# Three buffers for the splits of the down sums, their places, two units' sums in the FFN phase, and three halves of one input on VectorE

## The chip, the cores and the metric

The kernel runs on one core of a Trainium2 chip. The metric is the device time of one execution in microseconds; a kernel's time is the median of several runs. TensorE (PE) multiplies, VectorE (DVE), ScalarE (ACT) and GpSimd (POOL) work elementwise, and SyncE (SP) issues nearly all transfers. Each engine works its instructions off in the order in which the program gives them.

## The reference

Three steps follow one another: strided attention (4 batches, 8 heads, 576 positions, head size 64), a mixture of 8 experts whose gate is balanced by eight Sinkhorn rounds, and an FFN with a sigmoid gate. All in float32; the 2304 tokens are the rows of `x`, which are 512 wide.

```
def _moe_ref(x, w_gate, w1, w2):
    ...                                  # P: gate, balanced over tokens and experts
    for e in range(E):                   # E = 8, w1[e] 512 x 1024, w2[e] 1024 x 512
        h = np.maximum(x @ w1[e], 0.0)
        ye = h @ w2[e]
        out += P[:, e:e + 1] * ye

def _moe2_ref(x, w_in, w_out):           # 512 x 2048 and 2048 x 512
    h = x @ w_in
    g = h * (1.0 / (1.0 + np.exp(-1.702 * h)))
    return (g @ w_out).astype(np.float32)
```

## The kernel before, in words

**Blocks and phases.** The tokens are cut into three blocks of 768. The work behind the attention goes through six phases: MoE of block 0 (phase 0), MoE of block 1 (phase 1), FFN of block 0 (phase 2), MoE of block 2 (phase 3, "seven"), FFN of block 1 (phase 4), FFN of block 2 (phase 5). A phase is cut into units of 256 hidden columns: 32 units in a MoE phase (four an expert), 8 in an FFN phase. So units 0 to 31 are phase 0, 32 to 63 phase 1, 64 to 71 phase 2, 72 to 103 phase 3, 104 to 111 phase 4 and 112 to 119 phase 5.

**Products.** Float32 accuracy is had by splitting each operand into a high half (rounded to float32r by ScalarE) and a low half (the difference, made by GpSimd or VectorE), and adding three products. The product of a unit with its up weights is done by a scheme of seven smaller products in place of eight (PRODUCTS: X11, S1, S2, X12, S3, S4, X22), each six matmuls of 384 columns into a bank A, B or C. S1 to S4 are sums of quarters of the input (tiles `sa`, `sb`), T1 to T4 are sums of quarters of the weight. ScalarE copies some partial results out of the bank before the next product adds into it (`c`); after X11 that copy has to be done before product S2 goes on adding into bank A.

**Pieces.** A unit is 13 pieces: product 0, down tile 0, product 1, down tile 1 and so on to product 6. A down tile is six matmuls of 512 columns with the hidden values of the unit before. `side[piece_at(unit, k)]` holds the work of the other engines that is issued right behind piece k of a unit; a k of 13 or more is a piece of the next unit. Within one piece the order is that of the calls that filled it: `plan_weights` and `plan_inputs` come first, `plan_down_sums` late. The whole order is written out by hand; the tile framework only adds the waits.

**The weights of phase 3.** In phase 3 the down product too is done by the scheme of seven, and its weights come from a DRAM buffer `s7moe` (`sw7`), which is filled in phase 1. There `plan_down_sums` makes for every unit, from the down weights that the unit has loaded anyway (`raw`), four sums T1 to T4 on GpSimd (tile `dsums`, pieces 6 and 7), and splits each: high half on ScalarE, low half on GpSimd (tile `kw`, two buffers), then a store to `s7moe` by SyncE, one split at each of the pieces 8 to 11. A buffer of `kw` is free once its store has landed.

**Inputs of the next phase.** `plan_inputs` makes the split input `xc` of a phase during the last two units of the phase before: high halves on ScalarE, low halves on GpSimd; those numbered 1, 3 and 5, and the sums S3 and S4, are on VectorE for the phases of block 0 (`shared`). In phases 2 and 3 the results of the MoE are turned (`px`, four TensorE transposes and a ScalarE copy) into the input of a later FFN phase.

**FFN of block 0.** In phase 2 the FFN weights are new: GpSimd makes the four weight sums of the next unit (three instructions, L205 to L207) and the low halves of seven weight tiles and two down-weight tiles a unit, ScalarE their high halves. Later phases load them split.

**Phase 3's end.** Unit 104 carries its seven products and the last fourteen chains of phase 3's down product, whose inputs `comb` are split by ScalarE, VectorE and GpSimd and whose results VectorE adds into `sum`.

Of the kernel before, what the change touches and what calls it, by code (L numbers as in the profile page):

```python
# [8 lines left out]
F32 = mybir.dt.float32  # L9
F32R = mybir.dt.float32r  # L10
# [5 lines left out]
P = 128  # L16
# [26 lines left out]
PRODUCTS = (  # L43
    ("X11", "W11", "A", True, False),
    ("S1", "T1", "C", True, False),
    ("S2", "T2", "A", False, False),
    ("X12", "W21", "B", True, True),
    ("S3", "T3", "A", False, False),
    ("S4", "W22", "C", False, True),
    ("X22", "T4", "A", False, True),  # L50
)
NPR = len(PRODUCTS)
# [3 lines left out]
def strided_attention_moe_ffn(  # L56
# [13 lines left out]
    nc = tc.nc  # L70
    B, NPAIR, _, _, S = qk.shape
    NT, D = out.shape
# [25 lines left out]
    raws = ExitStack()  # L98
# [49 lines left out]
    side = defaultdict(list)  # L148
# [11 lines left out]
    FIRST_UNIT = []  # L160
# [10 lines left out]
    def seven(i):  # L171
        return S0 <= i < S1
# [4 lines left out]
    def piece_at(unit, k):  # L177
        return unit * PPU + k


    raw = {}
# [83 lines left out]

    SEVEN_FROM = NB - 2
    down_sums = {}

    def plan_down_sums(dp, i):

        n = UNITS[i][3]
        g = nc.gpsimd

        def q(k):
            return raw[2, i][:, k // 2, k % 2 * 2 * P : (k % 2 + 1) * 2 * P]

        def sums(m):
            if m == 0:
                down_sums[i] = dp.tile([P, 4, 2 * P], F32, tag="sums", name="dsums")
            t = down_sums[i]  # L280
            a, b = ((q(1), q(0)), (q(3), q(1)), (q(3), t[:, 0, :]), (q(2), t[:, 2, :]))[m]
            g.tensor_tensor(out=t[:, m, :], in0=a, in1=b, op=ALU.subtract)  # L282

        def split(k):
            t = dp.tile([P, 2, 2 * P], F32R, tag="kw", name="kw", bufs=2)
            src = down_sums[i][:, WHERE[PRODUCTS[k][1]][1], :]
            split_into(t, src, sw7[n, k].rearrange("p (h c) -> p h c", h=2))

        for m in range(4):
            side[piece_at(i, 6 + m // 2)].append(lambda m=m: sums(m))  # L290
        ks = [k for k in range(NPR) if PRODUCTS[k][1][0] == "T"]
        for m, k in enumerate(ks):
            side[piece_at(i, 8 + m)].append(lambda k=k: split(k))

    def plan_weights():

# [19 lines left out]
    def plan_sums(dp, i, lo, hi):  # L316

        r = {}

        def load():  # L320
            r["raw"] = dp.tile([P, 4, 2 * P], F32, tag="raws", name="raws")
            nc.sync.dma_start(out=r["raw"].rearrange("p q c -> p (q c)"), in_=wa[UNITS[i][3]])

        def sums():
            raw[1, i] = r["raw"]
            r["todo"] = sums_w1(i, dp)

        def split(k):
            t = dp.tile([P, 2, 2 * P], F32R, tag="kw", name="kw", bufs=2)
            split_into(t, quarter(i, PRODUCTS[k][1]), sw1["moe"][UNITS[i][3], k].rearrange("p (h c) -> p h c", h=2))  # L330

        tasks = [load, lambda: None, sums] + [lambda n=n: r["todo"][n]() for n in range(4)]
        tasks += [lambda k=k: split(k) for k in range(NPR) if PRODUCTS[k][1][0] == "T"]
        spread(tasks, lo, hi)
# [101 lines left out]
    def plan_inputs():  # L436

        v, g = nc.vector, nc.gpsimd
        for ph in range(1, len(PHASES)):
            last = FIRST_UNIT[ph] - 1  # L440

            shared = PHASES[ph][1] == 0
            low_v = (1, 3, 5) if shared else ()

            def put(unit, k, fn, *args):
                side[piece_at(unit, k)].append(lambda: fn(*args))

            put(last - 1, 6, input_sum, ph, 1, g)
            put(last - 1, 8, input_sum, ph, 2, g)
            put(last - 1, 9, input_high, ph, 0)  # L450
            put(last - 1, 10, input_low, ph, 0, v if 0 in low_v else g)
            for m in range(1, NPR):
                put(last, 2 * m - 1, input_high, ph, m)
                put(last, 2 * m - 1, input_low, ph, m, v if m in low_v else g)
                if m in (1, 2):
                    put(last, 2 * m, input_sum, ph, m + 3, v if shared else g)
# [152 lines left out]
    at = {p: [i for i, x in enumerate(groups) if x[:2] == p] for p in pairs}  # L609
# [480 lines left out]
    with tc.manual_schedule():  # L1090

        idle = hp.tile([P, NH], F32R, tag="hh22", name="idle", bufs=2)
        nc.vector.memset(f(idle), 0.0)
        idle_out = ps.tile([P, 512], F32, tag="y", name="idle_out", bufs=2)

        def keep_warm(n):
            for _ in range(n):
                nc.tensor.matmul(out=idle_out[:, :NH], lhsT=idle[:, :P], rhs=idle, start=True, stop=True)

        load_qk(0, PAIRS[0])  # L1100
        keep_warm(IDLE_FIRST)
        nc.scalar.dma_start(out=msk, in_=masks)
        load_qk(0, PAIRS[1])
        load_v(0, PAIRS[0])
        nc.scalar.dma_start(out=cst, in_=consts)
        load_w1(0)
        load_w2(0)
        nc.vector.memset(wgr, 0.0)
        nc.sync.dma_start(out=wgr[:, :, :E], in_=wg)

        plan_weights()
        plan_inputs()
        plan_kept()
        plan_turns()

        done = [0]

        def advance():
            g = done[0]
            pieces[g]()  # L1120
            for t in side.pop(g, ()):
                t()
            done[0] += 1

        quota = [0.0]
        load_w1(1)
        ahead = defaultdict(list)
        QUARTERS = ("W21", "W11", "W22", "W12")
        for n, what in enumerate(QUARTERS):
            ahead[5 + 2 * n].append(lambda what=what: split_plain(0, what))  # L1130
            ahead[12 + n].append(lambda what=what: split_plain(1, what))
        for ft in range(2):
            ahead[10 + ft].append(lambda ft=ft: split_w2(0, ft))
            ahead[17 + ft].append(lambda ft=ft: split_w2(1, ft))
        ahead[12].append(lambda: load_w1(2))
        ahead[12].append(lambda: load_w2(1))

        ahead[10].append(lambda: split_input(3))
        ahead[NHALF + 3].append(lambda: split_input(0))
        ahead[22].append(lambda: split_input(6))  # L1140
        ahead[NFIRST + 3].append(lambda: split_input("X21"))
        BY_HALF = 4 * PLAIN + 3 * (PLAIN - 1)

        def fill_first():
            quota[0] += IDLE_GAP
            keep_warm(int(quota[0]))
            quota[0] -= int(quota[0])

        def fill_half():
            quota[0] += RATE_HALF  # L1150
            if quota[0] >= 1 and done[0] < BY_HALF:
                advance()
                quota[0] -= 1
            else:
                keep_warm(1)

        def fill():
            quota[0] += RATE
            while quota[0] >= 1:
                advance()  # L1160
                quota[0] -= 1

        plan_first_sums()
        side[20].append(lambda: gate_logits(0))
        for i in range(NSTEP):
            if i == NHALF + 4:
                quota[0] = 0.0
            att_step(i, fill_first if i < NHALF + 4 else fill_half if i < NFIRST + 4 else fill)
            for t in ahead.pop(i, ()):
                t()  # L1170

        while done[0] // PPU % 2 or done[0] % PPU < 2:
            advance()
        early.close()
        late.append(ctx.enter_context(tc.tile_pool(name="late", bufs=1, space=bass.MemoryType.PSUM)))
        turn_of.clear()
        dp = raws.enter_context(tc.tile_pool(name="dp", bufs=1, reuse_waits="tile"))
        g = done[0]
        steps = gate_steps()
        assert g + len(steps) + 2 < piece_at(WAITING * UPE + 1, 0), (g, len(steps))  # L1180
        for n, s in enumerate(steps):
            side[g + n].append(s)
        plan_decode(dp, g + len(steps), piece_at(FIRST_UNIT[2] - 4, 0))
        for i in range(PLAIN):
            plan_sums(dp, i, piece_at(WAITING * UPE + 4 + 6 * i, 0), piece_at(WAITING * UPE + 9 + 6 * i, 0))
        for i in range(FIRST_UNIT[1], FIRST_UNIT[2]):
            plan_down_sums(dp, i)
        plan_seven()
        while done[0] < piece_at(S0, 0):
            advance()  # L1190
        raws.close()
        sp.append(ctx.enter_context(tc.tile_pool(name="sp", bufs=1, reuse_waits="tile")))
        while done[0] < len(pieces):
            advance()
# [81 lines left out]
```

## Time and profile before

| | |
|---|---|
| time, median of 3 runs | 2060.83 us (2059.45 to 2063.22) |
| profiled execution | 2060.84 us, its span 2059.1 us |
| TensorE busy | 1988.2 us (97%) |
| VectorE busy | 1359.1 us (66%) |
| GpSimd busy | 1181.9 us (57%) |
| ScalarE busy | 815.9 us (40%) |
| moved by transfers | 483.41 MB, mean 235 GB/s |

All times in rows are microseconds from the start of the span, unless marked ns. A row of the timeline shows an instruction's start, its duration, its engine and line, what it writes and reads, and in brackets how long the engine stood idle before it and what ended that. PEclk is the granted clock of TensorE as a share of 2.4 GHz.

### The profile page before, as it was taken

Reading aid. Unit: us, or ns where it says so; the run is one execution under the profiler, and the core shown is the slowest. Engines: PE = TensorE matmul, PEld = TensorE weight load, DVE = VectorE, ACT = ScalarE, POOL = GpSimd, SP = SyncE. Lnnn points to the kernel's source line nnn. Section 1 sums busy time; section 2 is a strip of 40 time slices with the busy share of each in tenths; the row PEclk is TensorE's granted clock in tenths of the full one; section 3 lists DMA queues with packets and bytes.
Section 4 is the critical chain, followed back from the end, with each engine's and each line's share of the span. In section 5 each row is a group of like instructions: output and inputs, shape, how many; then the busy total and the mean of one; then the engine's idle time right before and its main releaser. Section 6 shows DMA issues by size and latency. Waiting matters only on the chain.

```text
span 2059.1 us, 32151 instructions
## 1 busy us (share of the span) xinstructions
PE 1988.2 (97%) x10697; PEld 1784.7 (87%) x10697; DVE 1359.1 (66%) x2427; ACT 815.9 (40%) x2014; POOL 1181.9 (57%) x1201
## 2 busy tenths in 40 slices
PE   8999999999999999999999899999999999999999
PEld 6777789888988888888888779899999999888888
DVE  6776587888876666666665556665656666566656
ACT  6555434444443333333333355433333333333432
POOL 4465557888887555555555776665555555830300
PEclk9999999999999999999999999999999999999999
DMA  6355468687766888888887676687788788665653
GB/s 211 121 171 203 155 209 272 220 274 248 254 202 225 277 279 277 283 282 263 281 278 256 223 251 244 202 296 257 245 268 266 260 264 259 220 192 179 209 186 132
DMA packets 245684, 483.41 MB, mean 235 GB/s; under 512 B 25824, under 2 KB 56720, under 8 KB 244752
## 3 DMA queue, kind: packets, MB, share of 16 engines
q1 hardware_dynamic: 245232, 480.91, 70.6%
q8 instruction: 85, 1.39, 0.3%
q14 instruction: 79, 0.65, 0.1%
q10 hardware_dynamic: 288, 0.46, 0.1%
HBM read 322.91 MB, written 158.36 MB: 234 GB/s over the span
## 4 chain that ended last, share of the span: by engine, by line
PE 73%; POOL 8%; DMA 6%; DVE 5%; ACT 4%; issue 3%; SPq 1%; ACTq 0%; POOLq 0%; DVEq 0%
PE pA L719 19%; PE y L879 11%; PE pC L719 9%; PE y L950 8%; PE y L952 8%; PE y L951 8%; PE pB L719 5%; DMA s7moe<-kw 5%; POOL w L219 2%; POOL dsums L282 2%; POOL xc L423 2%; POOL kw L219 1%; ACT hh L755 1%; PE sc L496 1%; DMA s7moe<-w 1%
## 5 line engine op out<-in xcount | busy, mean ns | idle before, releaser
L719 PE MATMUL pA<-xc,w 128*128 128x384 f32 x2880 | 575.2, 339 | 35.9 <-ACT c L745 34.1
L719 PEld LDWEIGHTS pA<-xc,w 128*128 128x128 f32 x2880 | 508.2, 189 | 70.8 <-ACT c L745 47.9
L950 PE MATMUL y<-w,hh 128*128 128x512 f32 x1056 | 418.5, 396 | 10.3 <-DVE acc L969 3.8
L952 PE MATMUL y<-w,hl 128*128 128x512 f32 x1056 | 420.5, 398 | 1.4 <-DVE hl L758 0.7
L951 PE MATMUL y<-w,hh 128*128 128x512 f32 x1056 | 418.2, 396 | 0.2 <-POOL w L219 0.2
L219 POOL TENSOR_TENSOR w<-raw,w 128x256 fp32r<-128x256 f32 (+1 forms) x266 | 286.8, 1084 | 227.1 <-ACT w L218 198.8
L969 DVE SCALAR_TENSOR_TENSOR acc<-y,pr,acc 128x512 f32<-128x512 f32 x300 | 224.3, 748 | 168.3 <-PE y L952 167.2
L719 PE MATMUL pC<-xc,w 128*128 128x384 f32 x1464 | 296.2, 336 | 0.0
L879 PE MATMUL y<-comb,w 128*128 128x384 f32 x1344 | 269.2, 335 | 5.0 <-POOL comb L829 3.0
L719 PEld LDWEIGHTS pC<-xc,w 128*128 128x128 f32 x1464 | 259.4, 188 | 16.0 <-issue 0.7
L879 PEld LDWEIGHTS y<-comb,w 128*128 128x128 f32 x1344 | 236.7, 188 | 5.6 <-POOL comb L829 3.4
L952 PEld LDWEIGHTS y<-w,hl 128*128 128x128 f32 x1056 | 198.7, 188 | 47.0 <-DVE hl L768 2.7
L950 PEld LDWEIGHTS y<-w,hh 128*128 128x128 f32 x1056 | 199.3, 189 | 42.1 <-ACT hh L765 5.4
L951 PEld LDWEIGHTS y<-w,hh 128*128 128x128 f32 x1056 | 198.9, 188 | 25.1 <-POOL w L219 0.6
L829 POOL TENSOR_TENSOR comb<-s,comb 128x384 fp32r<-128x384 f32 x128 | 129.9, 1027 | 157.4 <-ACT comb L824 157.3
L890 DVE TENSOR_TENSOR sum<-y,sum 128x384 f32<-128x384 f32 x210 | 115.7, 552 | 131.2 <-PE y L879 131.2
L745 ACT ACTIVATE c<-pA 128x384 f32<-128x384 f32 x236 | 115.3, 489 | 214.6 <-PE pA L719 213.3
L219 POOL TENSOR_TENSOR kw<-dsums,kw 128x256 fp32r<-128x256 f32 x128 | 95.9, 758 | 100.3 <-ACT kw L218 100.2
L755 ACT ACTIVATE hh<-pB 128x384 fp32r<-128x384 f32 x124 | 61.1, 492 | 225.5 <-DVE pB L774 137.2
L719 PE MATMUL pB<-xc,w 128*128 128x384 f32 x708 | 143.2, 336 | 0.0
L219 POOL TENSOR_TENSOR w<-sums,w 128x256 fp32r<-128x256 f32 x152 | 122.5, 811 | 35.7 <-ACT w L218 35.5
L218 ACT ACTIVATE w<-raw 128x256 fp32r<-128x256 f32 (+1 forms) x266 | 136.0, 525 | 2.4 <-DMA raw<-wb 1.6
(142 smaller groups left out, 2641.5 us busy)
## 6 DMA issues: line engine op xcount, KB each, us to landing
w<-s1moe SPq DMA_DIRECT2D x448, 256.0 KB, 4.0
w<-s7moe SPq DMA_DIRECT2D x224, 256.0 KB, 4.0
s1moe<-w SPq DMA_DIRECT2D x216, 256.0 KB, 2.5
raw<-wb SPq DMA_DIRECT2D x64, 512.0 KB, 4.5
s7moe<-kw SPq DMA_DIRECT2D x128, 256.0 KB, 3.0
w<-s1ffn SPq DMA_DIRECT2D x112, 256.0 KB, 2.7
s7moe<-w SPq DMA_DIRECT2D x96, 256.0 KB, 3.3
raw<-wa SPq DMA_DIRECT2D x32, 512.0 KB, 4.5
```

What stands on the lines that cost most here:

```text
L218: nc.scalar.activation(out=t[:, 0, :], in_=src, func=AF.Copy)
L219: nc.gpsimd.tensor_tensor(out=t[:, 1, :], in0=src, in1=f(t[:, 0, :]), op=ALU.subtract)
L719: nc.tensor.matmul(out=o, lhsT=w[:, hw, kk * P : (kk + 1) * P], rhs=x[:, hx, kk, :], start=opens and m == 0, stop=ends and m == len(todo) - 1,
L745: nc.scalar.activation(out=t, in_=bank[b][:, :NH], func=AF.Copy)
L755: nc.scalar.activation(out=hh, in_=src, func=AF.Relu)
L829: eng.tensor_tensor(out=t[:, 1, :], in0=part[i, q], in1=f(t[:, 0, :]), op=ALU.subtract)
L879: nc.tensor.matmul(out=o, lhsT=t[:, hw, dt * P : (dt + 1) * P], rhs=x[:, hx, :], start=(n == 0), stop=(n == 5))
L890: nc.vector.tensor_tensor(out=a, in0=o, in1=a, op=ALU.add)
L950: nc.tensor.matmul(out=y, lhsT=hh[:, c], rhs=w[:, 0], start=(m == 0), stop=False)
L951: nc.tensor.matmul(out=y, lhsT=hh[:, c], rhs=w[:, 1], start=False, stop=False)
L952: nc.tensor.matmul(out=y, lhsT=hl[:, c], rhs=w[:, 0], start=False, stop=(m == 1))
L969: nc.vector.scalar_tensor_tensor(out=a, in0=y, scalar=p, in1=a, op0=ALU.mult, op1=ALU.add)
```

## The change

The tile `kw` gets a third buffer. Of a unit's four splits of down sums, each now stands two pieces behind the last (8, 10, 12, 14; the last is piece 1 of the next unit). For units 62 and 63 the sums are taken out of phase 1: the down weights are loaded once more (`raws`), at the start of unit 65 for unit 62 and of unit 67 for unit 63, the four sums are made at pieces 8 to 11 of that unit and the four splits at pieces 0, 3, 6 and 9 of the next. And `low_v` holds for a phase that follows phase 3 as well: in units 102 and 103 VectorE makes the low halves 1, 3 and 5 of phase 4's input, while its sums stay on GpSimd.

```diff
-    def plan_down_sums(dp, i):
+    down_raw = {}
+
+    def plan_down_sums(dp, i, again=None):
...
         def q(k):
-            return raw[2, i][:, k // 2, k % 2 * 2 * P : (k % 2 + 1) * 2 * P]
+            return down_raw.get(i, raw[2, i])[:, k // 2, k % 2 * 2 * P : (k % 2 + 1) * 2 * P]
...
         def split(k):
-            t = dp.tile([P, 2, 2 * P], F32R, tag="kw", name="kw", bufs=2)
+            t = dp.tile([P, 2, 2 * P], F32R, tag="kw", name="kw", bufs=3)
...
+        def load():
+            down_raw[i] = dp.tile([P, 2, D], F32, tag="raws", name="raws2")
+            nc.sync.dma_start(out=down_raw[i].rearrange("p q c -> p (q c)"), in_=wb[n])
+
+        ks = [k for k in range(NPR) if PRODUCTS[k][1][0] == "T"]
+        if again is not None:
+
+            side[piece_at(again, 0)].append(load)
         for m in range(4):
-            side[piece_at(i, 6 + m // 2)].append(lambda m=m: sums(m))
-        ks = [k for k in range(NPR) if PRODUCTS[k][1][0] == "T"]
+            at = piece_at(i, 6 + m // 2) if again is None else piece_at(again, 8 + m)
+            side[at].append(lambda m=m: sums(m))
         for m, k in enumerate(ks):
-            side[piece_at(i, 8 + m)].append(lambda k=k: split(k))
+            at = piece_at(i, 8 + 2 * m) if again is None else piece_at(again + 1, 3 * m)
+            side[at].append(lambda k=k: split(k))
...
-            low_v = (1, 3, 5) if shared else ()
+            low_v = (1, 3, 5) if shared or seven(last) else ()
...
         for i in range(FIRST_UNIT[1], FIRST_UNIT[2]):
-            plan_down_sums(dp, i)
+            left = FIRST_UNIT[2] - i
+            plan_down_sums(dp, i, FIRST_UNIT[2] + 5 - 2 * left if left <= 2 else None)
```

## Rows read from the trace of the kernel before

**Rows 1.** The page, busy time, share and instructions of each engine.
```profile
PE 1988.2 (97%) x10697; PEld 1784.7 (87%) x10697; DVE 1359.1 (66%) x2427; ACT 815.9 (40%) x2014; POOL 1181.9 (57%) x1201
```
**Rows 2.** Busy time by stretch: length, engines (instructions), TensorE clock, DMA share, GB/s.
```profile
312.91:438.03 125.12, 125.12 (x626) 112.47 (x626) 98.75 (x154) 53.59 (x130) 99.42 (x105) 1.00 0.76 255
641.79:1139.20 497.41, 468.76 (x2288) 411.98 (x2287) 315.84 (x521) 169.68 (x385) 282.38 (x312) 0.99 0.83 274
1139.20:1154.91 15.71, 15.71 (x79) 13.97 (x79) 7.88 (x13) 5.76 (x13) 8.30 (x10) 1.00 0.92 297
1154.91:1219.14 64.23, 50.36 (x235) 42.94 (x235) 34.33 (x50) 30.77 (x69) 52.82 (x55) 0.97 0.62 214
1251.77:1268.32 16.55, 16.55 (x88) 14.91 (x87) 11.08 (x19) 9.45 (x23) 10.84 (x13) 1.00 0.69 239
1344.20:1781.00 436.80, 436.80 (x2522) 436.80 (x2521) 269.78 (x512) 145.03 (x305) 251.00 (x246) 1.00 0.81 263
1781.00:1809.94 28.94, 23.97 (x127) 23.33 (x127) 13.88 (x26) 10.01 (x20) 23.38 (x18) 0.94 0.57 185
```
**Rows 3.** The same for the matmuls of line 719 alone (42 a unit).
```profile
641.79:1139.20 497.41, 245.08 (x1220) 216.57 (x1219) 0.99 0.83 274
```
**Rows 4.** Waits, units 33 to 61: total us, times, longest.
```profile
ACT kw L218 <- DMA s7moe<-kw: 130.9, 55, 5.0
...
PE pA L719 <- ACT c L745: 28.0, 25, 3.3
```
**Rows 5.** Timeline of ScalarE and of TensorE at the end of unit 43.
```profile
830.14 0.41 ACT L218 ACTIVATE kw<-dsums 128x256 fp32r<-128x256 f32 x1
...
835.23 0.42 ACT L218 ACTIVATE kw<-dsums 128x256 fp32r<-128x256 f32 x1 [2.44 <-DMA s7moe<-kw]
...
837.91 0.48 ACT L745 ACTIVATE c<-pA 128x384 f32<-128x384 f32 x1
...
838.45 1.33 PE L719 MATMUL pA<-xc,w 128*128 128x384 f32 x6 [0.76 <-ACT c L745]
```
**Rows 6.** Tile kw in units 33 to 61, its stores.
```profile
DMA to landing us min/median/max: 2.0/3.0/5.3
```
**Rows 7.** Waits of TensorE in units 63 to 65, and one GpSimd timeline row.
```profile
PE pA L719 <- ACT c L745: 5.7, 2, 3.7
PE y L950 <- DVE acc L969: 3.8, 2, 3.1
PE y L950 <- ACT hh L755: 3.0, 1, 3.0
...
1163.58 1.27 POOL L205 TENSOR_TENSOR sums<-raw 128x512 f32<-128x512 f32 x1
```
**Rows 8.** GpSimd by form, units 33 to 61: busy us, mean ns, idle before.
```profile
L219 POOL TENSOR_TENSOR kw<-dsums,kw 128x256 fp32r<-128x256 f32 x118 | 88.5, 759 | 94.4 <-ACT kw L218 94.4
...
L282 POOL TENSOR_TENSOR dsums<-raw 128x256 f32<-128x256 f32 x58 | 51.4, 905 | 0.0
```
**Rows 9.** Timeline of TensorE and GpSimd in unit 104.
```profile
1785.17 1.31 PE L879 MATMUL y<-comb,w 128*128 128x384 f32 x6 [1.93 <-DVE sum L890]
...
1797.50 2.46 PE L879 MATMUL y<-comb,w 128*128 128x384 f32 x8 [3.04 <-POOL comb L829]
...
1795.50 3.87 POOL L829 TENSOR_TENSOR comb<-s,comb 128x384 fp32r<-128x384 f32 x4
```
**Rows 10.** Timeline of VectorE and GpSimd at the end of unit 63.
```profile
1172.50 2.00 DVE L408 TENSOR_TENSOR sb<-z,sb 128x768 f32<-128x768 f32 x1 [3.14 <-POOL xc L423]
1174.42 0.74 DVE L969 SCALAR_TENSOR_TENSOR acc<-y,pr,acc 128x512 f32<-128x512 f32 x1
1175.08 0.94 DVE L423 TENSOR_TENSOR xc<-z,xc 128x768 fp32r<-128x768 f32 x1
...
1181.15 2.48 DVE L423 TENSOR_TENSOR xc<-sb,xc 128x768 fp32r<-128x768 f32 x1 [1.60 <-ACT xc L418]
...
1180.97 1.85 POOL L423 TENSOR_TENSOR xc<-sa,xc 128x768 fp32r<-128x768 f32 x1
```

More of the change, by code (lines that the diff above doesn't have):

```diff
@@ L328, in split @@
         def split(k):
-            t = dp.tile([P, 2, 2 * P], F32R, tag="kw", name="kw", bufs=2)
+            t = dp.tile([P, 2, 2 * P], F32R, tag="kw", name="kw", bufs=3)
             split_into(t, quarter(i, PRODUCTS[k][1]), sw1["moe"][UNITS[i][3], k].rearrange("p (h c) -> p h c", h=2))
```

## The prediction

> **What bounds the kernel now.** I read the page first: TensorE is busy 1988.2 of 2059.1 us [rows 1], so a gain can only come from its idle time and from the time after idling in which it runs slowly. I cut the span at the first product (X11) of each unit and compared stretches by engine [rows 2]; that they hold whole units shows in the number of product matmuls, 42 a unit [rows 3]. Eight units of phase 0 take 125.12 us with TensorE never idle: 15.64 us is what a full unit costs when nothing is late. Three stretches stand above that, and the diff touches all three:
> - Units 33 to 61 (phase 1): 497.41 us for 29 units. 29 x 15.64 = 453.56. Six input turns lie in it too; an FFN unit with two of them and no idle time takes 16.55, so six cost 3 x 0.91 = 2.73. Excess: 41.1 us, of which 28.65 is idle (497.41 - 468.76), the rest half-rate clock and refilling after the stalls.
> - Units 63 to 65: 64.23 us for three, excess 64.23 - 46.92 = 17.3, of which 13.9 idle, at a mean granted clock of 0.97.
> - Unit 104: seven plain products and fourteen chained ones, 126 matmuls. The thirty units of phase 3 have 84 each and take 436.80 / 30 = 14.56 us, so 21.84 would do; it takes 28.94. Excess 7.1, of which 4.97 idle, at a mean clock of 0.94.
>
> Then the waits of the first stretch, by releaser: ScalarE waits 130.9 us for stores of `kw` to land, TensorE 28.0 us for ScalarE's copy `c` [rows 4]. One unit shows how they join [rows 5]: of its four splits the third waits 2.44 us for a store, the fourth waits again, and `c<-pA`, ready long before, stands behind them; TensorE's product S2 adds into the bank that this copy must read first, and starts 0.76 late. A store lands in 2.0 to 5.3 us, median 3.0 [rows 6].
>
> **Change 1: three buffers, splits at pieces 8, 10, 12, 14.** Same instructions, other places and one buffer more. Buffers now go round in threes, so in a unit only the fourth split can meet the first one's store; the second and third take buffers whose stores were issued a unit earlier. The third split stands ahead of the next unit's `c<-pA` as before, but no longer waits; the fourth is now behind that copy. Where does its wait go? From the first split to the store having landed takes 5.1 us in the unit shown (830.14 to 835.23). In an unstalled unit a product takes 14.56 / 14 = 1.04 us and a down tile (15.64 - 7.28) / 6 = 1.39. S3 ends at 10.8; after a VectorE add and ScalarE's `hh<-pB` the first split starts at about 12.7, the fourth at 15.64 + 1.04 + 0.6 = 17.3: 4.6 us apart, so it waits about 0.5. Behind it on ScalarE stand `c<-pC`, `c<-pA` of S2 and the next down-weight split. TensorE first needs the second of these, for S3, 9.7 us into that unit, at 25.4; split and copies take 1.4, so the first store may land 25.4 - 1.4 - 12.7 = 11.3 us after its split began before TensorE waits. The wait is thus covered by 6 us. On SP the stores wait for GpSimd's half as before and pass the same loads; a `w` load behind them is due a unit later. POOL's splits come later in its order, after the sums that the second split waits for now. Bounds: nothing gained (every wait moves to the fourth split) to the whole 41.1. I take 40.0, near the upper end: 28.0 of the 28.65 us of idle time stand before that one copy [rows 4].
>
> **Change 2: units 62 and 63 lose their sums and splits.** Each loses four subtractions and four splits: on POOL at most 4 x 0.905 + 4 x 0.76 = 6.7 us a unit [rows 8], on ScalarE 1.7 and its waits. Of the stalls of units 63 to 65 [rows 7], two of 5.7 together are the copy behind `kw` and go. Two of 3.8 are down tiles behind VectorE's accumulation; that stood behind the sum S4, which waited for POOL to finish the low half of S2; POOL had begun unit 64's weight sums only at 1163.58, after the last `kw`. Now it begins them before unit 63 starts, and the low half ends about 7.7 us into the unit (four weight splits and 1.8 us behind ScalarE's copies); S4 (2.00 [rows 10]) and the accumulation (0.74) then end at 10.4, and the fifth down tile, which needs its bank, starts at 10.8. They go, by a hair. The 3.0 is `hh` of S4, behind the low half of the sixth input on VectorE (2.48); that stays, and I leave 1.5 us of it. The remaining 1.4 of the 13.9 (FFN unit 65) comes from POOL's sums being late in unit 64; they start some 7 us earlier in the unit (an estimate from the same order), so I leave 0.4. With 0.3 for the clock, 2.2 of 17.3 stay: 15.1 gained; bounds 5.7 (the copies alone) to 17.3.
>
> The work comes back in FFN units 65 to 68: two loads of 512 KB, eight sums and eight splits, on POOL 13.3 us, on ScalarE 3.3. An FFN unit leaves POOL 16.55 - 10.84 = 5.7 us free and ScalarE 7.1 [rows 2]; added are 3.0 to 3.6 and 1.7. What hides it is that slack, and that each weight split serves a unit later. With splits three pieces apart and three buffers no store is waited for. The sums delay the next unit's weight sums by some 2.3 us, which ScalarE reaches later still. I take 0.7 lost; bounds 0 and 13.3 (POOL's time in full).
>
> **Change 3: VectorE makes three low halves for the FFN of block 1.** (FFN of block 2 is not touched: its predecessor is no seven-product unit.) In unit 104 TensorE waits 3.04 for the second of four `comb` halves [rows 9], ready at 1797.44 (1795.50 + half of 3.87) and wanted 3.04 before the matmul's start. POOL works them off in order, and ahead of them are six low halves of this input. Three of 1.85 each [rows 10] leave POOL, so `comb` comes 5.5 earlier and this stall goes, with the slow clock after it: 3.04 of idle and most of 2.1. The other stall, 1.93 behind VectorE's `sum`, stays: POOL reaches S4 a little earlier, but VectorE now makes the sixth low half just ahead of that `sum` (0.94 alone, 2.48 beside POOL). I take 4.5; bounds -1.5 (POOL's gain eaten by new waits, and that `sum` later by 2.48 - 0.94 = 1.5) and 7.1.
>
> On that pair of durations the Trainium skill, page "SBUF — State Buffer", section "Who interferes with whom", says that a VectorE instruction with two SBUF inputs and a GpSimd one that reads SBUF share a port, and that the second to start stands still until the first is done. The trace agrees: the 2.48 us one began 0.2 after a POOL subtraction and ended 0.8 after it, and another took 0.94 [rows 10]. By this rule POOL would gain 5.5 - 3 x 0.94 = 2.7, `comb` would still be 0.3 late and the `sum` 1.2 later: 3.0 for change 3 instead of 4.5, 2003.4 in all.
>
> **Sum.** 40.0 + 15.1 - 0.7 + 4.5 = 58.9 us. The profiled execution took 2060.84 us (span 2059.1 and 1.7 around it), and the median of the runs is 2060.83, so no correction: 2060.8 - 58.9 = 2001.9, predicted 2002.
>
> **Rivals.**
> - *The transfers become the bound in phase 1.* The stretch moves 274 GB/s at a share of 0.83 [rows 2]; without its excess it would have to move 299 at 0.91. If 285, about halfway, were the most, 29 units would give back 456.3 x (299/285 - 1) = 22 us: 2024. Against: unit 62 alone moved 297 at 0.92 and took 15.71 without idle time. 10%.
> - *The FFN doesn't hide the moved work.* All 13.3 us of POOL in place of 0.7: 2014.5. For: POOL and ScalarE are in order, and two input turns a unit fall on ScalarE there. Against: the slack in rows 2. 10%.
> - *The spread cures half.* Stores land late beside the denser traffic, or another copy turns up behind the splits: 20 less in change 1, 2022. For: such a queue is what was found. 8%.
> - *Slower.* The fourth split's wait sits ahead of the copies of the next unit's S1 and S2. If the first split's store landed later than 11.3 us after the split, TensorE would stall in every unit. With the other gains of 18.9 the kernel is slower than before from (41.1 + 18.9) / 29 = 2.1 us a unit, a landing at 13.4; at 15 it would take 2060.8 + 29 x 3.7 - 60.0 = 2108. For: the store waits for POOL and shares SP with every load. Against: 5.1 in the unit shown, and no landing above 5.3 after its issue [rows 6]. 4%.
> - *Nothing happens*: the extra buffer isn't used as one, because the waits are kept on something coarser than a buffer. Then change 1 gives nothing: 2042. 3%.
>
> **Numbers.** My own case has 65%: 1995 (everything gained, 65.5 us) to 2010. The range, 1995 to 2020, takes in the FFN rival and part of the first and third. A measurement of this kernel tells 0.2% (4 us) from no change; only the slower rival and stray cases fall outside faster: 0.94 faster, 0.02 same, 0.04 slower.
>
> **What would show it.** Right: units 33 to 61 take 15.6 to 15.8 us each; ScalarE's waits for `kw` stores in them fall from 130.9 to under 25 us, and those left are on the fourth split; unit 63 takes under 17 us, unit 64 under 18.5, units 66 to 69 no more than 16.6; in unit 104 the wait for `comb` is gone and that for `sum` is there. Wrong: a stretch of phase 1 above 16.2 us a unit with TensorE waiting for anything, or idle time above 2 us in units 65 to 69.

## The result and the profile after

The changed kernel takes 2005.62 us (median of 4 runs, 2004.76 to 2007.75), the kernel before 2060.14 in the same comparison (2057.24 to 2063.22): a ratio of 0.9737, 95% interval 0.9720 to 0.9754. The forecast was 2002 in a range of 1995 to 2020. The profiled execution has a span of 2002.7 us, 56.4 less than before; 58.9 were forecast.

The stretches of the kernel after, cut at the first product of a unit as in [rows 2]; columns as there:

```profile
639.92:1097.18 457.26, 456.70 (x2287) 410.39 (x2287) 322.04 (x521) 173.35 (x384) 285.21 (x312) 1.00 0.88 298
...
1112.82:1164.41 51.59, 49.20 (x235) 43.32 (x235) 33.96 (x49) 28.00 (x61) 42.45 (x42) 0.97 0.66 231
...
1197.07:1213.61 16.54, 16.54 (x87) 14.90 (x87) 11.15 (x18) 10.61 (x27) 15.33 (x20) 1.00 0.75 262
...
1726.10:1754.02 27.92, 24.10 (x128) 23.03 (x127) 17.27 (x31) 9.98 (x20) 19.65 (x15) 0.94 0.60 196
```

The first row is units 33 to 61: 40.15 us shorter, and TensorE's idle time fell from 28.65 to 0.56 us. Transfers now move 298 GB/s in it. The second is units 63 to 65, 12.64 us shorter and still 4.7 above three full units. The third is FFN unit 68, with the moved splits in it: GpSimd is busy 15.33 of 16.54 us, and TensorE is never idle. The fourth is unit 104: only 1.03 us shorter.

Where the 56.4 us came from, by stretches (before less after): units 33 to 61 40.15; 63 to 65 12.64; 66 to 71 -0.70; 72 and 73 1.00; 103 and 104 0.90; behind 104 0.4; units 32 and 62 0.1; and 1.85 before unit 32, where both kernels do the same work. That last part is not the change's: 1.4 of it is there before the first product of unit 0, and over the thirteen profiles of the twelve kernels run here, which have the same work in their first 32 units, unit 32 begins between 623.5 and 626.4 us, with kernels of three buffers at both ends. What sets it is not known. Differences of under 3 us between kernels are therefore read below from their stretches.

The unit of [rows 5] in the kernel after, ScalarE's timeline at the end of unit 43:

```profile
813.13 0.41 ACT L218 ACTIVATE kw<-dsums 128x256 fp32r<-128x256 f32 x1
...
815.67 0.41 ACT L218 ACTIVATE kw<-dsums 128x256 fp32r<-128x256 f32 x1
...
816.35 0.42 ACT L218 ACTIVATE kw<-dsums 128x256 fp32r<-128x256 f32 x1
816.90 0.49 ACT L755 ACTIVATE c<-pA 128x384 f32<-128x384 f32 x1
818.22 0.42 ACT L218 ACTIVATE kw<-dsums 128x256 fp32r<-128x256 f32 x1 [0.83 <-DMA s7moe<-kw]
819.33 0.49 ACT L755 ACTIVATE c<-pC 128x384 f32<-128x384 f32 x1 [0.69 <-PE pC L729]
```

The third split runs straight through, the copy `c<-pA` follows it, and the wait is on the fourth split, behind the copy; the next copy still waits for TensorE (0.69 us), so TensorE is not held up by it. Over the stretch, the view of tile `kw` in the kernel after gives ScalarE's waits (us, times) and the landing of its stores:

```profile
  DMA s7moe<-kw: 28.2, 26
...
DMA to landing us min/median/max: 2.0/4.9/6.8
```

28.2 us of waits in place of 130.9 [rows 4], all on the fourth split, in 26 of the 29 units. The stores themselves land later than before, 4.9 us in the median against 3.0 [rows 6], and that does no harm.

### The profile page after: what moved, and what is told of

Its sections match the earlier page's. It is cut to its first block, busy times and chain, and to the rows that moved or that the text cites. A ratio compares the mean times of both kernels' runs of the same rounds, so it can differ in the third digit from the quotient of the medians.

```text
span 2002.7 us, 32174 instructions
## 1 busy us (share of the span) xinstructions
PE 1975.0 (99%) x10697; PEld 1783.6 (89%) x10697; DVE 1370.8 (68%) x2430; ACT 819.1 (41%) x2014; POOL 1180.9 (59%) x1198
## 4 chain that ended last, share of the span: by engine, by line
PE 86%; DVE 5%; POOL 4%; issue 2%; ACT 2%; DMA 1%; SPq 0%; POOLq 0%; ACTq 0%; DVEq 0%
PE pA L729 22%; PE pC L729 11%; PE y L889 11%; PE y L962 11%; PE y L960 11%; PE y L961 11%; PE pB L729 6%; POOL xc L433 1%; PE sc L506 1%; POOL w L219 1%; PE av L577 1%; PE pt L557 1%; PE idle_out L1108 1%; DVE hl L778 1%; DVE sg L774 0%
## 5 line engine op out<-in xcount | busy, mean ns | idle before, releaser
L729 PE MATMUL pA<-xc,w 128*128 128x384 f32 x2880 | 568.5, 336 | 2.1 <-DVE pB L803 1.7
L989 DVE TENSOR_TENSOR acc<-y,acc 128x512 f32<-128x512 f32 x126 | 86.5, 687 | 71.7 <-PE y L962 71.3
```

The costliest lines, as they stand in the source:

```text
L729: nc.tensor.matmul(out=o, lhsT=w[:, hw, kk * P : (kk + 1) * P], rhs=x[:, hx, kk, :], start=opens and m == 0, stop=ends and m == len(todo) - 1,
L989: nc.vector.tensor_tensor(out=a, in0=y, in1=a, op=ALU.add)
```

## The experiments

Lines of the kernel after and of all experiments are up to ten higher than in the kernel before. "Before" is the kernel before, "the changed kernel" the one after.

**Change 1 in its two parts.** First the buffer alone, against before (`plan_sums`, which also makes `kw` tiles, in phase 0, has the same edit):

```diff
-            t = dp.tile([P, 2, 2 * P], F32R, tag="kw", name="kw", bufs=2)
+            t = dp.tile([P, 2, 2 * P], F32R, tag="kw", name="kw", bufs=3)
```

> Before plus the third kw buffer alone: splits stay at pieces 8 to 11, units 62 and 63 and VectorE's halves as before. Theory (ScalarE's copy stands behind the waiting splits): the third split no longer waits; the fourth, at piece 11 and still ahead of the copy of X11, waits for the first one's store (some 5.3 us after that split, so until about 18.0 us into the unit); the copy then ends near 19.4 and S2 wants it at 20.5, so only late stores still stall. Units 33 to 61 take 458 to 466 us instead of 497.4, the time is about 2024 (2021 to 2030). Rival (places matter, the buffer does not): the fourth split stalls the copy as before, 485 us or more in that stretch, time 2048 or more.

Measured: 2023.22 us, ratio 0.9811 (0.9792 to 0.9831). Units 33 to 61, and TensorE's waits there:

```profile
641.99:1106.14 464.15, 458.83 (x2288) 409.77 (x2287) 323.87 (x521) 169.50 (x386) 286.02 (x312) 1.00 0.88 294
```
```profile
PE pA L729 <- ACT c L755: 4.8, 6, 1.5
```

The buffer alone gives 33.3 of the 40.2 us, with six stalls left at the same copy, as the theory had it. Then the places alone, with two buffers:

```diff
-            side[piece_at(i, 8 + m)].append(lambda k=k: split(k))
+            side[piece_at(i, 8 + 2 * m)].append(lambda k=k: split(k))
```

> Before plus the new places alone (8, 10, 12, 14) with two kw buffers. Theory: the third split, at piece 12 and ahead of the copy of X11, waits for the first one's store until about 18.0 us into the unit, the copy ends at about 19.0, S2 wants it at 20.5; the fourth is behind the copy. Little stalls: units 33 to 61 in 458 to 470 us, time about 2026 (2021 to 2034). Rival (the buffer is what counts): the third split blocks the copy nearly as before, 480 us or more, time 2043 or more.

Measured: 2034.06 us, ratio 0.9870 (0.9853 to 0.9886). The same stretch; TensorE's waits; and the longest waits of all engines:

```profile
642.23:1115.72 473.49, 462.50 (x2288) 410.34 (x2287) 327.43 (x521) 165.69 (x384) 285.30 (x312) 1.00 0.87 288
```
```profile
PE pA L729 <- ACT c L755: 10.2, 12, 2.2
```
```profile
ACT kw L218 <- DMA s7moe<-kw: 177.3, 57, 5.7
```

The places alone give 23.9 us: the stretch is 3.5 us longer than I allowed, the time lies at the end of its range, and both are far from the rival. The last row is the one to look at. ScalarE waits for stores 177.3 us here, more than the 130.9 of the kernel before, and the kernel is 27 us faster than the kernel before in the same comparison (2061.36). Sorted by split, the third waits 82 us in both kernels. The fourth waits 49 us ahead of the copy in the kernel before and 95 us behind it here. With the buffer alone, 81 us of waits stand ahead of the copy, all on the fourth split. The sum of an engine's waits is no measure of what they cost. And all of change 1, without changes 2 and 3:

> Before plus the whole of change 1 (three buffers and new places), without changes 2 and 3. Theory: units 33 to 61 in 457.3 us as in the changed kernel, units 63 to 65 lose the two stalls at the copy (5.7 us) but keep those behind the late low half: 56 to 60 us instead of 64.2; time about 2014 (2011 to 2020). Rival (the gain of the long stretch needs change 2, since with the sums of units 62 and 63 the queue is handed on): 465 us or more in the stretch.

Measured: 2017.55 us, ratio 0.9788 (0.9769 to 0.9806). Units 33 to 61 and units 63 to 65:

```profile
642.22:1099.45 457.23, 456.71 (x2287) 410.34 (x2287) 325.58 (x521) 174.37 (x384) 286.97 (x312) 1.00 0.89 298
1115.10:1175.95 60.85, 52.01 (x235) 44.11 (x235) 34.26 (x50) 29.94 (x68) 52.92 (x55) 0.94 0.65 224
```

The long stretch has its whole gain without change 2. Units 63 to 65 lose only 3.4 us by it, less than the 4 to 8 I gave it: with the copy out of the way, the wait behind the late low half grew instead, from 3.8 us [rows 7] to 6.0, and the granted clock over the three units fell from 0.97 to 0.94:

```profile
PE y L960 <- DVE acc L979: 6.0, 2, 3.7
```

**Change 2 alone**, on two buffers and the old places (its diff is that part of the change):

> Before plus change 2 alone (sums and splits of units 62 and 63 in the FFN phase), two buffers, old places, VectorE's halves as before. Theory: units 33 to 61 stay at 497 us, units 63 to 65 take 51.6 us as in the changed kernel, FFN units 66 to 69 no more than 16.6 each; time about 2047 (2044 to 2051). Rival (the FFN phase pays for the moved work): units 65 to 72 longer by 3 us or more in all, time 2051 or more.

Measured: 2050.05 us, ratio 0.9945 (0.9928 to 0.9962). Units 33 to 61, 63 to 65, and FFN units 66 to 69:

```profile
642.20:1141.54 499.34, 468.54 (x2288) 412.06 (x2288) 316.67 (x521) 169.63 (x385) 282.06 (x312) 0.99 0.83 273
1157.39:1209.00 51.61, 49.24 (x236) 43.12 (x236) 34.05 (x49) 27.99 (x61) 42.40 (x42) 0.97 0.69 238
1209.00:1274.28 65.28, 65.28 (x338) 58.81 (x338) 41.90 (x69) 39.10 (x95) 54.20 (x64) 1.00 0.80 283
```

Change 2 alone brings the whole 12.6 us of units 63 to 65, and FFN units 66 to 69 take 65.28 us, what they took before to the hundredth: in these units the moved work is hidden altogether, even with two buffers.

**Change 3 taken out of the changed kernel:**

```diff
-            low_v = (1, 3, 5) if shared or seven(last) else ()
+            low_v = (1, 3, 5) if shared else ()
```

> The changed kernel without change 3: GpSimd makes all low halves of the input for the FFN of block 1, as before. Theory: change 3 is worth only what unit 104 shows, some 1 us: unit 104 takes 28 to 29 us with its two waits (1.9 behind VectorE's sum, 1.4 to 3.0 for comb), all else as in the changed kernel, time about 2006.5 (2004 to 2010). Rival (the forecast: 4.5 us): 2010 or more. Second rival (what VectorE took over costs as much as it gives): 2004 or less.

Measured: 2007.05 us (2005.24 to 2010.63), ratio 0.9741 (0.9724 to 0.9759); the changed kernel's 0.9737 lies inside. Unit 104, and TensorE's waits in it:

```profile
1726.52:1754.49 27.97, 24.20 (x128) 23.28 (x127) 13.95 (x26) 10.01 (x20) 23.37 (x18) 0.94 0.59 193
```
```profile
PE y L889 <- DVE sum L900: 1.9, 1, 1.9
PE y L889 <- POOL comb L839: 1.5, 1, 1.5
```

27.97 without change 3, 27.92 with it. Without it the unit comes in two forms: 28.95 before, 28.99 and 28.93 in the runs of change 1 and of change 2 alone, but 27.97 to 28.10 here and in the first two experiments. `comb` releases TensorE 16.5 us into the unit in all six; the forms differ in where the slow clock falls (last section). With change 3 the unit takes 27.92, and in two later runs with the same program for it (the second low half, and the changed kernel once more):

```profile
1727.18:1753.95 26.77, 23.57 (x128) 23.22 (x127) 17.24 (x31) 9.96 (x20) 19.66 (x15) 0.94 0.61 196
1726.28:1754.50 28.22, 24.21 (x127) 23.28 (x127) 17.25 (x31) 9.96 (x20) 19.67 (x15) 0.94 0.59 189
```

On average that is 0.9 us less than the six without it, with the two groups overlapping; unit 103 gives 0.1 to 0.2 of it back (14.69 to 14.75 us against 14.56). So change 3 is worth less than 1 us.

**Which half costs on VectorE.** The changed kernel, with other halves on VectorE for the FFN of block 1. Two (1, 3):

```diff
-            low_v = (1, 3, 5) if shared or seven(last) else ()
+            low_v = (1, 3, 5) if shared else (1, 3) if seven(last) else ()
```

> The changed kernel, but for the FFN of block 1 VectorE makes the low halves 1 and 3 only, GpSimd the fifth again. Theory (the fifth stands on VectorE ahead of the sum that TensorE waits for): the wait for sum falls from 3.24 to 1.9 or less and the wait for comb stays away, GpSimd having had 1.65 us to spare; unit 104 takes 24 to 26.5 us instead of 27.9, time about 2003.5. Rival (the shared port slows VectorE whatever it works on): the wait for sum stays above 2.5. Second rival (GpSimd is late again): comb waits 1.4 or more, 28 us or more.

Measured: 2003.95 us, ratio 0.9724 (0.9708 to 0.9740). Unit 104 and TensorE's waits in it:

```profile
1727.61:1752.47 24.86, 22.68 (x128) 21.72 (x128) 16.43 (x30) 10.08 (x20) 20.66 (x16) 1.00 0.68 210
```
```profile
PE y L889 <- DVE sum L900: 1.9, 2, 1.1
PE y L889 <- POOL comb L839: 0.3, 1, 0.3
```

24.86 us: the waits for `sum` and `comb` are 1.1 us at most, and the granted clock is 1.00 over the unit. One, the first, with `(1,)` in that line:

> The changed kernel, but for the FFN of block 1 VectorE makes the first low half only. Theory: the wait for sum is below 1.9, since GpSimd reaches S4 one half earlier and nothing new stands ahead of the sum; comb comes 1.85 us earlier than with none, so it waits 0 to 1.2; unit 104 takes 24.5 to 27 us, time about 2004. Rival of the shared port: the wait for sum above 2.5 here as well. Rival of GpSimd: comb waits 1.4 or more.

Measured: 2006.40 us, ratio 0.9740 (0.9724 to 0.9756); the time missed its 2004, unit 104 took 26.72 us, as expected. The wait for `comb` is gone, but that for `sum` did not fall below 1.9:

```profile
1727.52:1754.24 26.72, 24.23 (x128) 23.30 (x127) 16.22 (x29) 9.49 (x20) 22.21 (x17) 0.94 0.63 201
```
```profile
PE y L889 <- DVE sum L900: 2.1, 2, 1.9
```

And the fifth alone, with `(5,)`:

> The changed kernel, but for the FFN of block 1 VectorE makes the fifth low half alone. Theory (the fifth, on VectorE ahead of the sum, is what costs): the wait for sum is 3 us or more although VectorE has two halves fewer, since GpSimd also reaches S4 no earlier; comb comes late or just in time; unit 104 takes 28 us or more, time 2005.5 to 2009. Rival (the number of halves beside GpSimd's work sets the cost, not which): the wait for sum is 2.2 or less and unit 104 takes 27 us or less, as with the first half alone.

Measured: 2009.78 us (2006.14 to 2011.01), ratio 0.9754 (0.9739 to 0.9769), 0.8 above the upper end. Unit 104, TensorE's waits in it, and VectorE's row of the fifth half:

```profile
1728.95:1759.41 30.46, 25.47 (x128) 24.35 (x127) 17.37 (x30) 10.01 (x20) 22.40 (x17) 0.89 0.55 179
```
```profile
PE y L889 <- DVE sum L900: 4.5, 2, 3.9
```
```profile
1730.81 1.67 DVE L433 TENSOR_TENSOR xc<-sb,xc 128x768 fp32r<-128x768 f32 x1 [3.58 <-ACT xc L428]
```

30.46 us, the slowest form of all with a single half moved. VectorE stands idle for 3.58 us ahead of that half, since ScalarE's high half is not there; ScalarE in turn waits for the sum S4, which GpSimd makes behind the other halves. Which half is moved decides, not how many: the fifth on VectorE costs, the first and third together give. The third alone was not run.

**The stall left in unit 63.** The changed kernel, and the second half on VectorE too for the FFN of block 0:

```diff
-            low_v = (1, 3, 5) if shared or seven(last) else ()
+            low_v = (1, 2, 3, 5) if ph == FIRST_UNIT.index(64) else (1, 3, 5) if shared or seven(last) else ()
```

> The changed kernel, and VectorE makes the second low half too for the FFN of block 0 (1, 2, 3, 5 in place of 1, 3, 5), so that its sum S4 no longer waits for GpSimd. Theory: the stall of 2.24 us behind VectorE's accumulation in unit 63 was GpSimd coming late with that half; it goes with the slow clock behind it, units 63 to 65 take 47.5 to 49.5 us instead of 51.6, time about 2002.5. Rival (VectorE's own queue is the limit, or the wait for the hidden value of S4 takes its place): 50.5 us or more.

Measured: 2004.73 us, ratio 0.9728 (0.9712 to 0.9744). Units 63 to 65, and TensorE's waits there:

```profile
1113.39:1164.35 50.96, 49.18 (x235) 43.40 (x235) 34.92 (x50) 28.11 (x61) 41.92 (x41) 0.97 0.68 235
```
```profile
PE y L960 <- ACT hh L765: 1.8, 1, 1.8
```

The rival holds: the wait behind the accumulation is gone, and one for S4's hidden value has taken its place; 0.6 us gained, not 3. Last, the fifth half back on GpSimd in both places:

```diff
-            low_v = (1, 3, 5) if shared or seven(last) else ()
+            low_v = (1, 2, 3) if shared else (1, 3) if seven(last) else ()
```

> The changed kernel, but VectorE makes the low halves 1, 2 and 3 for the FFN of block 0 and 1 and 3 for the FFN of block 1; GpSimd makes the fifth in both. Theory (each late half was on the engine that also makes what TensorE waits for): in unit 63 the wait behind the accumulation is gone as with 1, 2, 3, 5, and the wait for the hidden value of S4 (1.77 there) is gone too, since the fifth no longer stands ahead of S4's addition; units 63 to 65 take 46.9 to 48.5 us instead of 51.6, unit 104 24.5 to 26.8, time 1998 to 2001. Rival (GpSimd, one half heavier again, is late with weight sums or with the fourth and fifth half): 50.5 us or more in units 63 to 65, 2002.5 or more.

Measured: 2002.26 us (2001.08 to 2005.34), ratio 0.9723 (0.9708 to 0.9737). Units 63 to 65 and unit 104, and TensorE's waits in the first:

```profile
1115.29:1164.85 49.56, 47.90 (x236) 41.87 (x236) 33.09 (x49) 28.01 (x61) 43.20 (x42) 1.00 0.68 241
1726.95:1751.81 24.86, 22.70 (x127) 21.74 (x127) 16.47 (x30) 10.08 (x20) 20.65 (x16) 1.00 0.66 212
```
```profile
PE y L960 <- ACT hh L775: 1.4, 1, 1.4
PE y L962 <- DVE hl L778: 0.2, 1, 0.2
```

Neither theory: the first two waits are gone, but 1.65 us turn up in unit 65 at the first hidden value of the FFN, so 49.56 lies between the two forecasts. The kernel before has a stall of 1.4 us at the same place in unit 65; what brings it back here is not shown. The ratio is the lowest of all runs, but level with the 0.9724 of the halves 1 and 3. The changed kernel itself, beside it on the same chip:

> The changed kernel itself once more, on the chip of the two others, for comparison: all theories 2005.6 us (2003.5 to 2007.5), unit 104 with the wait for sum of 3.2 and no wait for comb; units 63 to 65 in 51.6 us.

Measured: 2006.40 us (2004.94 to 2008.04), ratio 0.9739 (0.9725 to 0.9753). The two intervals overlap; by the stretches the version without the fifth half is 2.05 us shorter in units 63 to 65 (49.56 against 51.61) and 3.4 in unit 104 (24.86 against 28.22). Its span is only 2.6 us shorter because its unit 32 begins 2.8 us later, where both do the same work.

## Why the prediction was right, and where it was off

The changed kernel lies 3.6 us above the predicted time, inside the likeliest case's own range. That it came so near is in part luck: the stretches for which I had terms gave 53.1 us (40.15, 12.64, 1.03, and -0.7 in units 66 to 71) where they should have given 58.9, and the other 3.3 of the 56.4 came from stretches for which I had none, 1.85 of them from before unit 32. By its steps:

- **Change 1, 40.0 us: 40.15.** The wait moved to the fourth split and behind the copy, at 1.0 us a unit (28.2 over 29) where 0.5 was worked out, and is hidden. That the order on ScalarE was the mechanism, and not the length of its waits, is shown by the places alone: more waiting, 27 us less time. ScalarE's waits for stores fell to 28.2 us, a little above the 25 that I set as the mark. Of the 12.5 us of excess that were not idle time, the mean clock of 0.99 [rows 2] makes only some 5 (an estimate, 0.01 of 497.41); the "refilling" that was to be the rest was not measured.
- **The rival of the transfers fell.** The stretch moves 298 GB/s and TensorE idles 0.56 us in it; a ceiling of 285 is not there. Stores land 1.9 us later in the median, which the fourth split's covered wait takes up.
- **Change 2, 15.1 us: 12.64.** The step that failed is "Now it begins them before unit 63 starts". GpSimd's timeline around the start of unit 63 (1112.82) in the kernel after:

```profile
1110.64 1.85 POOL L414 TENSOR_TENSOR sb<-sa,z 128x768 f32<-128x768 f32 x1
1112.45 1.84 POOL L433 TENSOR_TENSOR xc<-z,xc 128x768 fp32r<-128x768 f32 x1
1114.25 1.30 POOL L205 TENSOR_TENSOR sums<-raw 128x512 f32<-128x512 f32 x1
...
1121.38 1.86 POOL L433 TENSOR_TENSOR xc<-sb,xc 128x768 fp32r<-128x768 f32 x1
```

  I had freed GpSimd of the `kw` work and forgotten what else stands ahead: the sums and first low half of the new input, three instructions of 1.85 us that begin late in unit 62 (the last two are shown). The weight sums start 1.43 us into unit 63, the low half of S2 ends at 10.4 us in place of 7.7, and TensorE waits 2.24 us where I saw 0.4 to spare. Unit 63 took 19.75 us, above its mark of 17. The wait as the view gives it:

```profile
PE y L960 <- DVE acc L979: 2.2, 1, 2.2
```

  The 1.5 us that I left for the hidden value of S4 is there where that wait is removed (1.8), or where the clock stays up (1.3).
- **The moved work, -0.7 us: 0.0** in units 66 to 69, with change 2 alone and in the changed kernel. GpSimd is busy 4.5 us longer in unit 68 (15.33 after 10.84) where I gave it 3.0 to 3.6; that is 93% of the unit, and costs nothing there. But units 70 and 71 take 32.15 us in place of 31.44. Neither change 1 alone (31.50) nor change 2 alone (31.46) does that, only the two together, in every run that has both. So the 0.7 was lost after all, at a place that the prediction did not name; its cause stays open.
- **Change 3, 4.5 us: less than 1.** The step that failed is that the other stall "stays". `comb` did come in time, as forecast; but the wait for VectorE's `sum` grew from 1.93 to 3.24, and the slow clock that was to go with the `comb` stall fell behind this one: the granted clock over the unit is 0.94, as before. TensorE's wait in the kernel after; VectorE's timeline; and GpSimd's row beside it:

```profile
PE y L889 <- DVE sum L900: 3.4, 2, 3.2
```
```profile
1726.95 2.00 DVE L433 TENSOR_TENSOR xc<-sb,xc 128x768 fp32r<-128x768 f32 x1 [0.50 <-ACT xc L428]
1728.88 0.55 DVE L784 TENSOR_TENSOR pC<-pC,c 128x384 f32<-128x384 f32 x1
...
1729.94 0.55 DVE L900 TENSOR_TENSOR sum<-y,sum 128x384 f32<-128x384 f32 x1
```
```profile
1726.00 2.14 POOL L433 TENSOR_TENSOR xc<-sa,xc 128x768 fp32r<-128x768 f32 x1
```

  The fifth half waits for ScalarE and takes 2.00 us, and the addition of S4 and the `sum` stand behind it. I had seen this ("VectorE now makes the sixth low half just ahead of that `sum`") and charged nothing for it; my lower bound held it. (It is the half of product index 5, the sixth input.) The runs with one half and with two settle it: the fifth alone makes the wait 3.9 us; the first alone leaves it at 1.9, the first and third together make it two waits of 1.1 at most.
- The Trainium skill's rule of the shared port ("SBUF — State Buffer", "Who interferes with whom") gave 3.0 us for this change and so came nearer than I did. The trace agrees with it again: the half took 2.00 us and ended 0.8 after GpSimd's subtraction, where one took 0.94 before [rows 10]. Its 1.2 us for the `sum`, for which I gave no working, were 1.3, while `comb` was not late by its 0.3. But the number of halves beside GpSimd's work did not set the cost, their place in VectorE's queue did; the port only lengthened it.

## What to carry to other kernels

A wait of an in-order engine costs what stands behind it: before adding a buffer, ask what is queued behind the waiting instruction and whether the wait can be moved behind that. When work is taken off an engine, read its whole queue up to the instruction that you want early, not only the part that leaves. When work is shared out to a second engine, look which of its results TensorE waits for next: two halves moved gave 3 us or more in unit 104, the third took most of that back.

## What the runs showed of the hardware that was not expected

The clock did not fall alike after like stalls. In one execution of the changed kernel the stall of 2.24 us in unit 63 went with a lower clock (first fence, units 63 and 64), in another the stall of 2.23 did not (second fence):

```profile
1112.82:1132.57 19.75, 17.51 (x79) 15.38 (x79) 13.29 (x16) 9.68 (x20) 17.00 (x15) 0.91 0.50 170
1132.57:1148.35 15.78, 15.78 (x80) 13.96 (x79) 10.30 (x17) 9.64 (x21) 13.61 (x15) 1.00 0.65 221
```
```profile
1112.50:1130.66 18.16, 15.93 (x79) 14.04 (x79) 11.71 (x16) 9.69 (x20) 15.40 (x14) 1.00 0.50 156
1130.66:1148.04 17.38, 16.07 (x79) 13.92 (x79) 11.88 (x17) 9.65 (x21) 15.15 (x16) 1.00 0.67 225
```

The two units take 35.53 and 35.54 us together: where the clock stayed up, TensorE ran ahead into the wait for S4's hidden value (1.3 us), which the slow clock had covered. So a slow stretch ahead of a wait that was due anyway cost nothing here. Of the seven profiles with this stall (2.21 to 2.24 us), three have a granted clock of 0.91 over unit 63 (a part of it at 1.2 GHz, the rest at 2.4) and four of 1.00. What decided it stays open.

Unit 104 without change 3 shows the price of the other place. The unit's stretch up to the end of the wait for `comb`, and from there to the unit's end, in the kernel before (first fence) and in the changed kernel without change 3 (second fence):

```profile
1781.00:1797.50 16.50, 11.53 (x66) 10.89 (x65) 6.19 (x11) 6.54 (x13) 16.34 (x14) 1.00 0.61 199
1797.50:1809.94 12.44, 12.44 (x62) 12.44 (x63) 7.69 (x15) 3.47 (x7) 7.04 (x5) 0.86 0.53 165
```
```profile
1726.52:1743.04 16.52, 13.11 (x66) 12.47 (x65) 6.19 (x11) 5.90 (x12) 16.36 (x14) 0.90 0.60 198
1743.04:1754.49 11.45, 11.10 (x63) 10.81 (x63) 7.76 (x15) 4.11 (x9) 7.01 (x5) 1.00 0.57 185
```

Ahead of the wait the lower clock cost nothing (16.52 us against 16.50; the wait itself is 1.5 in place of 3.0). Behind it, where nothing was waited for any more, it cost 1.0 us (12.44 against 11.45).

Stores of 256 KB landed the later, the more the core moved: over units 33 to 61 the median was 3.0 us at 274 GB/s (before) and 3.1 at 273 (change 2 alone), 3.4 at 288 (the places alone), 3.7 at 294 (the buffer alone), and 5.1 and 4.9 at 298 (change 1, and the changed kernel). The longest, between 5.3 and 8.1, follow no such order. That the rate is the cause is not shown, since the places and buffers differ as well.
